# A fused attention and two-MLP kernel: a planner that counts the landing of stores, new ranks, and a warm-up on the identity

## The chip, the core and the metric

The program runs on one core of a Trainium2 chip. The metric is the device time of one execution in microseconds (us), and the kernel's figure is the median of several runs. A core has TensorE (PE) for matrix products, VectorE (DVE), ScalarE (ACT) and GpSimd (POOL) for elementwise work, and SyncE (SP), whose instruction queue issues all the transfers here. Each engine takes its own instructions strictly in the order in which they were written and waits on semaphores that the others raise. PE's results go to PSUM banks, everything else lives in SBUF.

## What is computed

```python
# q, k, v: (4 batches, 8 heads, 576 tokens, 64)
rel  = pos[:, None] - pos[None, :]
mask = (rel >= 0) & (rel < 128)                  # window of 128
s    = where(mask, q @ k.T / 8 - slope[h] * abs(rel), -1e9)
p    = exp(s - max(s)); p /= sum(p) + 1e-9
x    = (p @ v) laid out as (2304 tokens, 512)
a, b = x @ w1, x @ w2                            # 512 -> 1024
y    = (a * b) @ w3 @ w_out                      # 1024 -> 1024 -> 512
h    = maximum(y @ w_in, 0)                      # 512 -> 2048
out  = (h * h) @ w_out2                          # 2048 -> 512, fp32
```

The weights arrive as 64-bit words, and the kernel makes fp32 of them itself.

## The kernel before

**Attention** runs over 16 pairs of heads. For a pair, `qk` loads two heads of q and k and four small loads fetch v (`t_load_v`, L395). PE makes the scores (L467, two groups a pair), DVE adds the bias and takes the row's extreme (`l_min`, L435), ACT takes the exponential (L443), DVE sums and inverts (L452, L453), the rows are normalized (L254 on DVE, L252 on POOL, L256 on ACT), PE transposes them against the identity in four groups (L503), ACT copies these to SBUF (`pt`, `pl`, by the helper at L200), and PE multiplies with v (L527, then L543). Batch 0's result stays in SBUF as a high and a low half, the other batches' results are stored to `x_scr`.

**Weights.** A weight tile of 1024 KB is loaded into one of 11 buffers with the tag `u` (those of w_out into four others), and three operations make fp32 of it: ACT L330, DVE L339 (or ACT L335) and DVE L345. w3 and w_out are multiplied with each other first (64 products, L659), so that y needs one product less. The eight tiles of w1 and w2 (`w12`) are then split into a high and a low half (L200 or L260, then L203) and also stored to `m_scrc` for later. The sixteen tiles of the second MLP's weights (`in_w2io`, L843) are merged in the same manner ahead of their use: load into `u`, conversion, store to `m_scri` or `m_scro` (L849).

**Products.** Each fp32 product is three products of halves (L195 to L197). For batch 0 there are 32 units of a and b (12 matmuls of 288 columns each; `ab`) and 16 units of y. A product of a and b (L722) is split into halves too (L260, L203: `gf`, `gt`). For batches 1 to 3 and for the second MLP the products go by seven block products instead of eight (L1080 to L1082, L1131 to L1133), with sums on DVE and copies on ACT. Their first one is L1080.

**What sets the order.** Nothing is written in program order by hand. `Plan` holds some 3,100 tasks, each with a rank, the engines it may run on with a cost for each, the tasks it depends on, and the buffers it takes and gives back. `Plan.run` goes through a modelled time: of the tasks that could start within 0.1 us of the earliest it takes that of the lowest rank, puts it on an engine, and notes when its buffers come free. A dependent task on another engine starts `lat` later (3.0 for a transfer). The result is the order of every engine's instructions. On the chip only this order is left: the waits are semaphores. A buffer that a store reads is given back by the store's task (`gives`), and the tile framework makes the next user of that buffer wait for the store to have landed. Where the plan finds PE idle for over 1 us in the first 40 us, it puts in matmuls whose result nobody reads (`filler`), and it opens with a few of them (`warm`, L569).

```python
            for h in gives:
                left[h] -= 1
                last[h] = max(last[h], fin)
                if left[h] == 0:
                    pool[self.holds[h][0]].append(last[h] + 0.1)
```

Of the kernel before, what the change touches and what calls it, by code (L numbers as in the profile page):

```python
# [12 lines left out]
ALU = mybir.AluOpType  # L13


RANK = dict(w34=3, h0=-20, w12=35.93, w12s=7.96, w12l=7.68, mg=500, mgs=4, yl=8, yn=0, hs=10)
B, H, S, D = 4, 8, 576, 64
NT = B * S
DM = H * D
# [13 lines left out]
class Plan:  # L33
# [22 lines left out]
    def add(self, name, rank, where, fn, deps=(), takes=(), gives=(), keep=0):  # L56

        assert name not in self.tasks, name
        self.tasks[name] = (rank, where, fn, tuple(deps), tuple(takes), tuple(gives), keep)

    def run(self):
        tasks = self.tasks
        need = {n: len(t[3]) for n, t in tasks.items()}
        users = {}
        for n, t in tasks.items():
            for d in t[3]:
                users.setdefault(d, []).append(n)

        pool = {tag: [0.0] * c for tag, c in self.caps.items()}
        left = {h: v[1] for h, v in self.holds.items()}  # L70
        last = {h: 0.0 for h in self.holds}
        free = {}
        lock = 0.0
        end, on = {}, {}
        ready = {n for n, c in need.items() if c == 0}
        order = []
        shape = lambda n: 1 if n[:3] == "pvl" else {"qk": 1, "pv": 2}.get(n[:2], 0)
        now = 0
        while ready:
            cands = []  # L80
            for n in ready:
                rank, where, fn, deps, takes, gives, keep = tasks[n]
                t0 = 0.0
                ok = True
                for tag in {self.holds[h][0] for h in takes}:
                    p = sorted(pool[tag])
                    want = sum(self.holds[h][0] == tag for h in takes)
                    if len(p) < want + keep:
                        ok = False
                        break  # L90
                    t0 = max(t0, p[want - 1])
                if not ok:
                    continue
                best = None
                for q, w in where.items():
                    e = q.lower()
                    if e == "pe" and shape(n) != now:
                        w += self.SWITCH
                    elif e == "pe" and now:
                        rank -= self.STAY  # L100
                    t = max(t0, free.get(e, 0.0))
                    if q in "Dp":
                        t = max(t, lock)
                    for d in deps:
                        t = max(t, end[d] + (0.0 if on[d] == e else self.lat[on[d]]))
                    key = t + w + self.bias.get(q, 0.0)
                    if best is None or (key, t) < best[:2]:
                        best = (key, t, q, w)
                cands.append((best[1], rank, n, best[2], best[3]))
            assert cands, (sorted(ready)[:20], {h: (v[0], left[h]) for h, v in self.holds.items() if left[h] > 0 and any(h in tasks[n][4] for n in end)})  # L110
            t0 = min(c[0] for c in cands)
            near = [c for c in cands if c[0] <= t0 + self.LOOK]
            t, rank, n, q, w = min(near, key=lambda c: (c[1], c[0], c[2]))
            e = q.lower()
            _, _, fn, deps, takes, gives, _ = tasks[n]
            if e == "pe":
                now = shape(n)
                idle = t - free.get(e, t)
                if 1.0 < idle and t < self.FILL:
                    for tag in "tg":  # L120
                        p = pool[tag]
                        if p and min(p) <= free[e]:
                            p.remove(min(p))
                            k = f"fill{len(order)}"
                            tasks[k] = (0, {}, lambda e, tag=tag, idle=idle: self.filler(tag, int((idle - 0.4) / 0.24), 128), (), (), (), 0)
                            order.append((k, e, free[e], t - 0.4))
                            p.append(t)
                            break
            ready.remove(n)
            for h in takes:  # L130
                p = pool[self.holds[h][0]]
                p.remove(min(p))
            fin = t + w
            end[n], on[n] = fin, e
            free[e] = fin
            if q in "Dp":
                lock = fin
            for h in gives:
                left[h] -= 1
                last[h] = max(last[h], fin)  # L140
                if left[h] == 0:
                    pool[self.holds[h][0]].append(last[h] + 0.1)
            order.append((n, e, t, fin))
            for u in users.get(n, ()):
                need[u] -= 1
                if need[u] == 0:
                    ready.add(u)
        assert len(order) == len(tasks) and len(end) + sum(n[:4] == "fill" for n in tasks) == len(tasks), [n for n in tasks if n not in end][:20]
        return order
# [3 lines left out]
def fused_kernel(  # L153
# [11 lines left out]
    nc = tc.nc  # L165
# [50 lines left out]
    ident = const.tile([128, 128], F32, name="ident")  # L216
    make_identity(nc, ident)

    bw = at.tile([128, H, 256], F32, name="bw")
# [65 lines left out]
    def w_dma(kb, n=1):  # L285
        return max(0.55 * n, kb / 300.0)
# [18 lines left out]
    w34 = [None] * 4  # L305
# [89 lines left out]
    def t_load_v(m):  # L395
        b, p = divmod(m, H // 2)
        v = vt[m % 2]
        nc.sync.dma_start(
            out=v[:, :, 0:4, :].rearrange("p h c d -> p h (c d)"),
            in_=v_main[b, 2 * p:2 * p + 2].rearrange("h p c -> p h c"),  # L400
        )
        nc.sync.dma_start(
            out=v[64:128, :, 4:6, :].rearrange("p h c d -> p h (c d)"),
            in_=v_main[b, 2 * p:2 * p + 2, 0:64, 2 * D:4 * D].rearrange("h p c -> p h c"),
        )
        nc.sync.dma_start(out=v[0:64, :, 4, :], in_=v_main[b, 2 * p:2 * p + 2, 64:128, 0:D].rearrange("h p d -> p h d"))
        nc.sync.dma_start(out=v[0:64, :, 5, :], in_=v_rest[b, 2 * p:2 * p + 2].rearrange("h p d -> p h d"))
# [155 lines left out]
        b, p = divmod(m, H // 2)  # L563
        nc.sync.dma_start(out=x_scr[b][p], in_=xt[b, p])

    def p_warm(tag="t", k=4, w=256):
        t = (ps_t if tag == "t" else ps_g).tile([128, 512], F32, tag=tag, name=tag)
        for _ in range(k):
            nc.tensor.matmul(t[:, 0:w], ident, bw[:, 0, 0:w], start=True, stop=True)  # L569

    plan.filler = p_warm

# [5 lines left out]
    def add_pair(m, rank):  # L578
# [8 lines left out]
        for n in heads:  # L587
            add(f"ldq{n}", r, {"dma": w_dma(295)}, lambda e, n=n: t_load_qk(n), [f"ldq{n - 1}"] if n else [],
                [f"qk{m}"] if n % 2 == 0 else [])
        add(f"ldv{m}", r + 0.1, {"dma": w_dma(393, 2)}, lambda e: t_load_v(m), [f"ldq{heads[1]}"], [f"v{m}"])  # L590
        for n in heads:
            hold(f"s0_{n}", "s", 3)
            hold(f"s1_{n}", "s", 2)
# [879 lines left out]
```

## Time and profile before

| what | value |
|---|---|
| median of 3 runs | 838.32 us (836.11 to 838.72) |
| the profiled execution | 835.16 us, its span 833.4 us |
| PE busy | 804.7 us (97%) |
| DVE busy | 610.1 us (73%) |
| ACT busy | 469.3 us (56%) |
| transfers | 138.73 MB, mean 166 GB/s |
| KB of one load or store | q and k of a head 288, v of a pair 256 + 64 + 32 + 32, a weight tile 1024, x_scr 288, m_scr 512 |

The span is the traced part of the execution; 1.8 us of the profiled execution lie around it. A busy PE is not PE at its peak, since matmuls overlap and their ends are modelled; a stage is better read by how many units of known length it got through.

### The profile page before, as it was taken

How to read it: one execution, taken by the hardware profiler on the slowest of the kernel's cores; microseconds unless marked ns; L12 is line 12 of the kernel's file. 1: busy time of each engine (PE TensorE's matmuls, PEld its weight loads, DVE VectorE, ACT ScalarE, POOL GpSimd, SP SyncE). 2: the span in 40 equal slices, each digit the busy share in tenths (PEclk: the TensorE clock that was granted, in tenths of full speed). 3: DMA queues.
4: the chain of work that ended last, by engine and by line, in shares of the span. 5: the costliest groups of instructions: out<-in, count | busy, mean ns of one | idle time of the engine just before them, and what ended most of it. 6: DMA issues, size and time to landing. Idle time of an engine off the chain costs nothing.

```text
span 833.4 us, 17233 instructions
## 1 busy us (share of the span) xinstructions
PE 804.7 (97%) x6716; PEld 748.0 (90%) x6716; DVE 610.1 (73%) x1349; ACT 469.3 (56%) x1011; POOL 63.3 (8%) x74
## 2 busy tenths in 40 slices
PE   6999999987999999999999999999999899999998
PEld 5655659876999999999999999999999899999998
DVE  5997899983598897797489574622599898676762
ACT  5877788873332452342234475645798776566531
POOL 1010010000000200020030130000112010000000
PEclk9999999998999999999999999999999999999999
DMA  9899899876732534202133453533795755544300
GB/s 252 275 317 286 271 299 283 245 203 198 237 123 93 171 139 160 73 1 76 52 109 105 155 184 129 190 114 112 246 291 199 206 142 158 139 135 140 93 26 32
DMA packets 96960, 138.73 MB, mean 166 GB/s; under 512 B 10864, under 2 KB 74864, under 8 KB 94832
## 3 DMA queue, kind: packets, MB, share of 16 engines
q1 hardware_dynamic: 96880, 137.65, 52.9%
q8 instruction: 52, 0.85, 0.4%
q14 instruction: 28, 0.23, 0.1%
HBM read 95.81 MB, written 41.81 MB: 165 GB/s over the span
## 4 chain that ended last, share of the span: by engine, by line
PE 80%; DMA 8%; DVE 6%; ACT 3%; issue 1%; SPq 1%; POOL 0%; POOLq 0%; ACTq 0%; DVEq 0%
PE xa L1131 8%; PE xa L1133 8%; PE xa L1132 8%; PE g L659 6%; PE g L195 5%; PE g L196 5%; PE g L197 5%; PE xb L1133 4%; PE xb L1131 4%; PE xb L1132 4%; DMA m_scri<-u 3%; PE al L1080 3%; PE al L1082 3%; PE al L1081 3%; PE s L467 2%; DMA u<-in_w2io_dram 2%
## 5 line engine op out<-in xcount | busy, mean ns | idle before, releaser
L1192 DVE TENSOR_TENSOR D<-xb,D 128x384 f32<-128x384 f32 (+1 forms) x66 | 34.0, 518 | 58.4 <-PE xb L1133 30.1
L195 PE MATMUL g<-gt,wu 128*128 128x288 f32 x256 | 76.7, 300 | 0.0
L196 PE MATMUL g<-gt,wu 128*128 128x288 f32 x256 | 76.3, 298 | 0.0
L197 PE MATMUL g<-gt,wu 128*128 128x288 f32 x256 | 76.1, 297 | 0.0
L443 ACT ACTIVATE e<-e,st 128x128 f32<-128x128 f32 (+1 forms) x144 | 62.5, 438 | 13.7 <-DVE st L435 13.1
L200 ACT ACTIVATE D<-xa 128x384 f32<-128x384 f32 (+1 forms) x102 | 46.2, 454 | 38.5 <-PE xa L1133 35.2
L659 PE MATMUL g<-raw 128*128 128x512 f32 x128 | 61.0, 603 | 0.0
L1080 PE MATMUL al<-x,wc 128*128 128x288 f32 x192 | 57.1, 297 | 1.3 <-ACT d L200 1.3
L203 DVE TENSOR_TENSOR ww<-fq,ww 128x1024 fp32r<-128x1024 f32 x34 | 41.6, 1222 | 22.1 <-ACT ww L200 21.9
L200 ACT ACTIVATE ww<-fq 128x1024 fp32r<-128x1024 f32 x35 | 37.0, 1058 | 34.9 <-PE xa L1133 19.3
L1082 PE MATMUL al<-x,wc 128*128 128x288 f32 x192 | 56.7, 295 | 0.0
L1081 PE MATMUL al<-x,wc 128*128 128x288 f32 x192 | 56.6, 295 | 0.0
L200 ACT ACTIVATE ye<-g 128x288 f32<-128x288 f32 x32 | 13.1, 411 | 69.8 <-PE g L197 62.3
L1222 ACT ACTIVATE D<-D 128x384 f32<-128x384 f32 x72 | 37.0, 523 | 24.9 <-DVE D L1192 24.7
L868 DVE TENSOR_TENSOR st<-st 128x256 f32<-128x256 f32 (+1 forms) x105 | 41.7, 427 | 10.9 <-DMA st<-m_scrc 5.9
L196 PEld LDWEIGHTS g<-gt,wu 128*128 128x128 f32 x256 | 48.9, 191 | 0.0
L197 PEld LDWEIGHTS g<-gt,wu 128*128 128x128 f32 x256 | 48.8, 191 | 0.0
L195 PEld LDWEIGHTS g<-gt,wu 128*128 128x128 f32 x256 | 48.6, 190 | 0.1
L503 PEld LDWEIGHTS t<-ident,e 128*128 128x128 f32 x208 | 24.4, 142 | 26.0 <-ACT pt L200 15.9
L200 ACT ACTIVATE d<-al 128x288 f32<-128x288 f32 x71 | 28.8, 409 | 31.4 <-PE al L1082 25.2
L503 PE MATMUL t<-ident,e 128*128 128x128 f32 x208 | 36.0, 286 | 8.9 <-ACT pt L200 8.8
L435 DVE CUSTOM_DVE_ANT_0 e<-s,bw 128x192 f32<-128x192 f32 (+1 forms) x128 | 40.9, 351 | 4.8 <-PE s L467 4.5
(270 smaller groups left out, 2783.6 us busy)
## 6 DMA issues: line engine op xcount, KB each, us to landing
s_scr<-D SPq DMA_DIRECT2D x96, 192.0 KB, 2.0
u<-in_w2io_dram SPq DMA_DIRECT2D x22, 512.0 KB, 6.1
fo<-s_scr SPq DMA_DIRECT2D x20, 512.0 KB, 4.9
qk<-in_qk_dram SPq DMA_DIRECT2D x32, 288.0 KB, 5.7
st<-m_scrc SPq DMA_DIRECT2D x18, 512.0 KB, 3.7
raw<-in_w3t_dram SPq DMA_DIRECT2D x8, 1024.0 KB, 8.7
raw<-in_w_dram SPq DMA_DIRECT2D x8, 1024.0 KB, 7.2
fq<-s_scr SPq DMA_DIRECT2D x16, 512.0 KB, 5.0
```

Of the source, the lines that this page charges most:

```text
L195: nc.tensor.matmul(o, wh, xh, start=start, stop=False)
L196: nc.tensor.matmul(o, wh, xl, start=False, stop=False)
L197: nc.tensor.matmul(o, wl, xh, start=False, stop=stop)
L200: nc.scalar.activation(out=o, in_=i, func=ACTF.Copy)
L443: nc.scalar.activation(out=e, in_=e, func=ACTF.Exp, bias=st[:, 0, x:x + 1], scale=-1.0, accum_out=st[:, 1, x:x + 1],)
L659: nc.tensor.matmul(gw[fi], wl, wr, start=c == 0, stop=c == 7)
L1080: nc.tensor.matmul(o, wh, xh, start=start and c == 0, stop=False, skip_group_check=True)
L1081: nc.tensor.matmul(o, wh, xl, start=False, stop=False, skip_group_check=True)
L1082: nc.tensor.matmul(o, wl, xh, start=False, stop=c == 1, skip_group_check=True)
L1131: nc.tensor.matmul(o, wh, xh, start=start, stop=False, skip_group_check=True)
L1132: nc.tensor.matmul(o, wh, xl, start=False, stop=False, skip_group_check=True)
L1133: nc.tensor.matmul(o, wl, xh, start=False, stop=stop, skip_group_check=True)
```

## The change

Four things are edited. In `RANK`, the first pair's rank goes from -20 to -40 and the step from pair to pair from 10 to 7, so that each pair ranks lower (earlier) against the weights. In `Plan.run`, a task on the `dma` engine gives its buffers back at its end plus `lat` plus 0.5, that is 3.5 later. The four loads of v are priced as three instead of two. The matmuls of `p_warm` read the identity on both sides, 128 columns wide, instead of the identity and the bias table; the opening ones are nine of 128 columns instead of four of 256.

```diff
-RANK = dict(w34=3, h0=-20, w12=35.93, ..., yl=8, yn=0, hs=10)
+RANK = dict(w34=3, h0=-40, w12=35.93, ..., yl=8, yn=0, hs=7)
...
-                            tasks[k] = (0, {}, lambda e, tag=tag, idle=idle: self.filler(tag, int((idle - 0.4) / 0.24), 128), (), (), (), 0)
+                            tasks[k] = (0, {}, lambda e, tag=tag, idle=idle: self.filler(tag, int((idle - 0.4) / 0.24)), (), (), (), 0)
...
-                last[h] = max(last[h], fin)
+                last[h] = max(last[h], fin + (self.lat[e] + 0.5 if e == "dma" else 0.0))
...
-    def p_warm(tag="t", k=4, w=256):
+    def p_warm(tag="t", k=9):
         t = (ps_t if tag == "t" else ps_g).tile([128, 512], F32, tag=tag, name=tag)
         for _ in range(k):
-            nc.tensor.matmul(t[:, 0:w], ident, bw[:, 0, 0:w], start=True, stop=True)
+            nc.tensor.matmul(t[:, 0:128], ident, ident, start=True, stop=True)
...
-        add(f"ldv{m}", r + 0.1, {"dma": w_dma(393, 2)}, lambda e: t_load_v(m), [f"ldq{heads[1]}"], [f"v{m}"])
+        add(f"ldv{m}", r + 0.1, {"dma": w_dma(393, 3)}, lambda e: t_load_v(m), [f"ldq{heads[1]}"], [f"v{m}"])
```

As a result the order moves as a whole up to the first L1080. Before, the 64 products L659 lay among pairs 2 to 9 and sixteen units of a and b and five of y among pairs 9 to 15. Now the L659 lie among pairs 3 to 15, and all units of a, b and y of batch 0 behind the last pair. From the first L1080 on, PE's order is the same but for some exchanged neighbours in the last third.

SP's queue before, in the attention's last pairs (`u` is a weight buffer, `m_scri` the store of a merged tile, `x_scr` an attention result, `v0`, `v1` and `qk` loads for the next pairs):

```order
L393 DMA qk_2098<-in_qk_dram 64x2x576 x2
L849 DMA m_scri0_95<-u_1889 128x1024
L843 DMA u_2183<-in_w2io_dram 128x1024 x2
L564 DMA x_scr2_89<-pt_2046 128x576
L398 DMA v1_162<-in_v_main_dram 128x2x256
L402 DMA v1_162<-in_v_main_dram 64x2x128
L406 DMA v1_162<-in_v_main_dram 64x2x64
L407 DMA v1_162<-in_v_rest_dram 64x2x64
L393 DMA qk_2294<-in_qk_dram 64x2x576 x2
L849 DMA m_scri1_96<-u_1977 128x1024
L843 DMA u_2355<-in_w2io_dram 128x1024 x2
```

SP's queue of the changed kernel, at its first loads of these tiles (`xm` is the load of a whole batch of attention results for batch 1):

```order
L370 DMA m_scrc7_110<-raw_2338 128x1024
L843 DMA u_2433<-in_w2io_dram 128x1024 x2
L564 DMA x_scr3_90<-pt_2342 128x576
L843 DMA u_2489<-in_w2io_dram 128x1024 x2
L843 DMA u_2543<-in_w2io_dram 128x1024 x2
L849 DMA m_scri0_95<-u_2433 128x1024
L1027 DMA xm_2612<-x_scr1_88 128x4x576
L849 DMA m_scri1_96<-u_2489 128x1024
L849 DMA m_scri2_97<-u_2543 128x1024
L843 DMA u_2692<-in_w2io_dram 128x1024 x2
L843 DMA u_2738<-in_w2io_dram 128x1024 x2
```

Before, a load that reuses the buffer of a store stood right behind that store, with loads for the next pairs behind it; now all loads of v, q and k stand ahead of the first L843, and three stores are issued before the next load that needs one of their buffers.

DVE before, around the second sum of the last pair (L452, L453; `u` a tile of the second MLP, `gf` and `gt` the product of a and b and its halves):

```order
L722 TENSOR_TENSOR gf<-g,a_sb 128x288
L260 CAST gt<-gf 128x288
L203 TENSOR_TENSOR gt<-gf,gt 128x288
L339 TENSOR_SCALAR u<-u 128x1024
L452 TENSOR_SCALAR st_164<-st_164 128x5
L453 RECIPROCAL st_164<-st_164 128x5
L254 TENSOR_SCALAR e<-e,st_164 128x128
L254 TENSOR_SCALAR e<-e,st_164 128x192 x4
L345 SCALAR_TENSOR_TENSOR u<-u 128x1024
```

DVE of the changed kernel at the same sum (`raw` and `wu` a tile of w1 and w2 and its halves or a half of w3 times w_out):

```order
L339 TENSOR_SCALAR raw<-raw 128x1024
L345 SCALAR_TENSOR_TENSOR raw<-raw 128x1024
L260 CAST wu<-raw 128x1024
L203 TENSOR_TENSOR wu<-raw,wu 128x1024
L452 TENSOR_SCALAR st_164<-st_164 128x5
L453 RECIPROCAL st_164<-st_164 128x5
L203 TENSOR_TENSOR wu<-g,wu 128x512
L254 TENSOR_SCALAR e<-e,st_164 128x192
L339 TENSOR_SCALAR raw<-raw 128x1024
L345 SCALAR_TENSOR_TENSOR raw<-raw 128x1024
```

Eight triples L722, L260, L203 and four conversions of `u`, which stood ahead of this sum, now stand behind it, and two more tiles of w1 and w2 are converted behind it.

## Rows read from the trace of the kernel before

**Rows 1.** Busy time by stage: window, PE, PEld, DVE, ACT, POOL, granted clock, DMA, GB/s
```profile
0.00:60.00 60.00, 51.28 (x595) 34.10 (x596) 47.35 (x190) 44.80 (x141) 6.72 (x22) 1.00 0.93 283
60.00:160.00 100.00, 99.89 (x1190) 68.37 (x1189) 89.31 (x334) 79.37 (x245) 4.39 (x6) 1.00 0.91 277
160.00:217.30 57.30, 47.82 (x568) 43.36 (x566) 31.42 (x108) 29.42 (x90) 0.00 (x0) 0.94 0.70 210
217.30:239.80 22.50, 22.50 (x169) 22.50 (x170) 19.34 (x38) 7.29 (x14) 0.00 (x0) 1.00 0.52 184
239.80:300.00 60.20, 58.87 (x438) 57.97 (x437) 55.40 (x111) 24.21 (x51) 6.01 (x5) 1.00 0.41 135
...
597.00:660.00 63.00, 59.07 (x354) 57.69 (x353) 56.65 (x79) 50.81 (x82) 9.89 (x10) 1.00 0.74 237
```

**Rows 2.** Waits in SP's queue, 0 to 200 us: us in total, times, longest
```profile
SPq L843 <- DMA m_scri<-u: 21.3, 4, 6.2
```

**Rows 3.** The chain that ended last, 140 to 225 us: start us, us, what
```profile
194.23 7.10 DMA m_scri<-u
```

**Rows 4.** ACT in order of time, 199 to 203 us
```profile
200.05 1.10 ACT L330 ACTIVATE u<-u 128x1024 f32<-128x1024 f32 x1 [4.97 <-DMA u<-in_w2io_dram]
```

**Rows 5.** PE's waits, 180 to 222 us
```profile
PE t L503 <- ACT pt L200: 6.3, 3, 3.7
```

**Rows 6.** PE by stretches of 2 us: window, PE busy, granted clock, DMA, GB/s
```profile
202.00:204.00 2.00, 2.00 (x10) 0.50 0.00 0
```

**Rows 7.** PE in order of time, 239.3 to 240.1 us
```profile
239.79 0.29 PE L1080 MATMUL al<-x,wc 128*128 128x288 f32 x1
```

**Rows 8.** DVE's waits, 10 to 190 us
```profile
DVE e L435 <- PE s L467: 10.8, 11, 3.9
DVE u L339 <- DMA u<-in_w2io_dram: 3.9, 2, 2.6
DVE raw L345 <- ACT raw L330: 2.7, 2, 2.2
DVE u L345 <- DMA m_scri<-u: 2.3, 1, 2.3
```

**Rows 9.** PE in order of time: the opening matmuls
```profile
4.95 3.78 PE L569 MATMUL t<-bw,ident 128*128 128x256 f32 x8 [4.95 <-POOL bw L229]
```

**Rows 10.** POOL and DVE in order of time, first 24 us
```profile
1.16 0.30 POOL masks.py:199 TENSOR_SCALAR_AFFINE_SELECT ident<-ident 128x128 f32<-128x128 f32 x1
...
10.33 0.29 DVE L435 CUSTOM_DVE_ANT_0 e<-s,bz 128x128 f32<-128x128 f32 x1 [3.90 <-PE s L467]
```

**Rows 11.** Transfers issued in the first 2.1 us: KB each, median us to landing
```profile
qk<-in_qk_dram SPq DMA_DIRECT2D x2, 288.0 KB, 4.3
```

**Rows 12.** DVE in order of time: second sums of pairs 9 and 15
```profile
124.98 0.16 DVE L452 TENSOR_SCALAR st<-st 128x5 f32<-128x5 f32 x1
...
190.58 0.16 DVE L452 TENSOR_SCALAR st<-st 128x5 f32<-128x5 f32 x1
```

**Rows 13.** DVE, 60 to 190 us, by shape: busy us, mean ns of one
```profile
L345 DVE SCALAR_TENSOR_TENSOR raw<-raw 128x1024 uint32<-128x1024 uint32 x12 | 14.7, 1223 | 3.0 <-ACT raw L330 2.7
...
L203 DVE TENSOR_TENSOR wu<-raw,wu 128x1024 fp32r<-128x1024 f32 x7 | 8.6, 1223 | 1.0 <-ACT wu L200 0.9
...
L339 DVE TENSOR_SCALAR raw<-raw 128x1024 uint32<-128x1024 uint32 x10 | 6.9, 691 | 0.0
...
L203 DVE TENSOR_TENSOR gt<-gf,gt 128x288 fp32r<-128x288 f32 x8 | 3.7, 459 | 0.3
L722 DVE TENSOR_TENSOR gf<-g,a_sb 128x288 f32<-128x288 f32 x8 | 3.6, 454 | 0.1
...
L260 DVE CAST gt<-gf 128x288 fp32r<-128x288 f32 x8 | 2.5, 310 | 0.3
```

**Rows 14.** PE in order of time: the end of pair 9's products with v
```profile
132.27 0.51 PE L543 MATMUL a<-pt,v 64*64 64x64 f32 x18
```

**Rows 15.** The page: GB/s in 40 slices of 20.8 us
```profile
GB/s 252 275 317 286 271 299 283 245 203 198 237 123 93 171 139 160 73 1 76 52 109 105 155 184 129 190 114 112 246 291 199 206 142 158 139 135 140 93 26 32
```

More of the change, by code (lines that the diff above doesn't have):

```diff
@@ L13 @@
 ALU = mybir.AluOpType
-RANK = dict(w34=3, h0=-20, w12=35.93, w12s=7.96, w12l=7.68, mg=500, mgs=4, yl=8, yn=0, hs=10)
+RANK = dict(w34=3, h0=-40, w12=35.93, w12s=7.96, w12l=7.68, mg=500, mgs=4, yl=8, yn=0, hs=7)
 B, H, S, D = 4, 8, 576, 64
```

## Prediction

> **What bounds the kernel now.** I read the busy time by stage first. From 217.3 us on the program is one dense row of matmuls: PE is busy all of 22.5 us, 58.9 of 60.2, and in the worst later stage 59.1 of 63.0 [rows 1]. What there is to win lies before. The first 60 us have PE at 51.3 of 60, and the stretch from 160 to 217.3 at 47.8 of 57.3 with a granted clock of 0.94 on average [rows 1]. All four edits act there.
>
> Why PE stops in the second stretch is read from the queues. SP's own waits show four loads of the second MLP's weights that stood 21.3 us in all for a store out of the same buffer, 6.2 the longest [rows 2]; the chain has such a store landing after 7.10 us [rows 3]. Behind a waiting load stand the loads of v, q and k of the next pairs. ACT then comes to the conversion of that tile, 4.97 us idle for its load [rows 4], and behind this conversion on ACT stands the copy of the transposed rows, without which PE can't go on: PE waits 6.3 us on it, 3.7 once [rows 5]. After that wait the granted clock is 0.50, that is 1.2 instead of 2.4 GHz [rows 6]. So one task that the plan believed free held three engines. The first block product L1080, behind which the order stays as it is, starts at 239.79 [rows 7]; the forecast is made for this instant.
>
> The runner-up is DVE. From 60 to 160 us it is busy 89.3 of 100 while PE is at 99.9 [rows 1], and what it waits for from 10 to 190 is 10.8 us for scores, 2.7 for ACT, and 3.9 + 2.3 for tiles of the second MLP or their stores [rows 8].
>
> **The change part by part.**
>
> The warm-up. PE's first matmul waits 4.95 us for the bias table and the opening takes 3.78 us for 1024 columns [rows 9]; the scores follow at 8.73. The identity is ready at 1.16 + 0.30 = 1.46 [rows 10]. Nine matmuls of 128 columns are 1152, at the same pace 4.25 us, so they end at 5.7. The two loads of q and k, issued in the first 2.1 us, take 4.3 us to land [rows 11]; I take 6.1 for the second. So the scores start some 2.6 us earlier, and DVE's first bias, at 10.33 after a wait of 3.90 [rows 10], with them. Bounds: 0 if something else is late, 3.9 if all of the wait goes. The fillers keep their size and reading the identity instead of the table is the same form, so I cost that at nothing; PE's idle time hides it.
>
> The ranks, the landing and the price of v work together through the order. DVE sets the pace of the attention, so I count what DVE does ahead of the second sum of pair 15, at 190.58 now [rows 12]. Behind this sum go eight triples L722, L260, L203 at 0.454 + 0.310 + 0.459 = 1.223, that is 9.8 us; four conversions of second-MLP tiles at 0.691 + 1.223 = 1.914, 7.7 us; two of w1 and w2, 3.8 us; and one low half, 1.22 us [rows 13]. That is 22.5. Two small drains and four small sums move too; against them nine normalizations come ahead of it, partly from POOL, and I set these off against each other.
>
> Waits of DVE. The 3.9 + 2.3 = 6.2 us on second-MLP tiles [rows 8] go, since no such load or conversion is left ahead of the last pair. Of the scores' 10.8, 3.9 were the start, so 6.9 + 2.7 = 9.6 stay open. Scores rank ahead of L659 more often now, but PE is needed nearly as much as DVE: ahead of pair 15's end it loses only 16 units of a and b and five of y, at 22.5 / 14 = 1.607 us each [rows 1] 33.7 us. Bounds: 0, and twice 9.6. I take 6, nearer to the row than to nothing, a gain of 3.6.
>
> So the sum of pair 15 comes at 190.6 - 2.6 - 22.5 - 6.2 - 3.6 = 155.7. What follows is a pair's tail: in pair 9, undisturbed, the second sum is at 124.98 [rows 12] and the products with v end at 132.27 + 0.51 = 132.8 [rows 14], 7.8 us, and one last L659 makes it 8.7: 164.4. Then batch 0 in one piece: 32 units of a and b and 8 of y. Forty such units take 64.3. L1080 starts at 228.7, 11.1 us earlier than now.
>
> In this piece DVE does what was put off: 16 triples (19.6), eight conversions (15.3), two of w1 and w2 with their halves, and the first operands of batch 1, some 55 us of 73. It is covered, but the eight second-MLP tiles now have to be loaded, converted and stored within those 64 us. SP's first such load waits for a store of w1 and w2 two rows ahead, and its fourth for the first merged store, three stores earlier. The landings leave one to four us to the conversions on ACT, so I take 0 here and 12.9 as the far bound (the loss of 160 to 217.3, below).
>
> After L1080 PE's order is the same. In 239.8 to 300 DVE is busy 55.4 of 60.2 [rows 1], but it has the same work left as before and meets it in the same order. The exchanged neighbours near 597 to 660, where PE loses 3.9 us in all [rows 1], I cost at 0, bounds 3.9 gained and 3.9 lost.
>
> The sum: 835.16 - 11.1 = 824.1 for an execution like the profiled one. The median of the runs shown is 3.2 us above it, so the forecast is 838.3 - 11.1 = 827.2.
>
> Two rules bear on this. A store of 512 KB took 7.10 us here [rows 3]. The Trainium skill, DMA: Bandwidth & Descriptors, section Anatomy of one DMA — SWDGE (gpsimd) path, gives about 2.0 us plus the bytes at 436 GB/s, an estimated 3.2 us for this one, on another issue path. By that figure the waits that go would be worth half, and the forecast 830; the measurement decides.
>
> The clock stays at 1.00 in the first 60 us with PE busy 51.3 of 60 [rows 1] and falls to 0.50 only after the 3.7 us wait [rows 5, 6]. The Trainium skill, TensorE: Matmul & The Clock Gate, section on the HAM clock gate, has idle time bring TensorE back to 1.2 GHz, which speaks against giving PE fewer products among the first pairs. Should it fall there, ten us at the lower level would cost five and leave 832; by the rows it doesn't.
>
> **The rivals.**
>
> More is gained. If PE is never late for DVE, the other 6 us go too: 821. For it: the first pairs have almost nothing but their own matmuls ahead of their scores. Against it: PE's own work up to that point is nearly as long as DVE's.
>
> The loads set the pace. Pairs are now asked for sooner. Ahead of pair 8's q and k the queue holds eight pairs' q and k, seven v, four tiles of w3, four of w_out and one store, 16.8 MB with them; the three first slices, at 252, 275 and 317 GB/s, moved 17.6 MB in 62.5 us [rows 15]. DVE wants these scores at about 65 us. If the queue's waits for buffers cost it a tenth to a fifth of that rate, the attention comes 6 to 11 us later: 833 to 838. The trace shows the queue blocked often, but with more bytes ahead.
>
> The stall moves instead of going. Loads of the second MLP's tiles wait for stores in the dense piece too, and behind them on SP stand the stores of y, whose two buffers PE needs. If they come late, ACT stands at a conversion ahead of its copies exactly as now. The price is what it costs now: 57.3 - 47.8 = 9.5 us idle and 0.06 x 57.3 = 3.4 us of clock, 12.9 [rows 1]. With the waits of DVE kept in full (3.6) that is 827.2 + 16.5 = 844, slower. It decides from the point where a tile lands more than about four us after the copy ahead of its conversion.
>
> The gain is given back. Batch 1's stage hangs on DVE, and if its weights or loads come no sooner, PE waits there for what it won: 836 to 840.
>
> **How the numbers follow.** The forecast has 50%, with its own range from 822 to 832; more gained 20%, the loads 14%, the gain given back 7%, the stall moved 9%. The range that leaves out no more than 2 in 10 runs from 816 (no waits, the whole 3.9 at the start, and the late stage's idle time gone) to 838 (the loads at their worst). A measurement of this kernel can tell about 0.3%, 2.5 us, from no change. Faster takes the first two and most of the loads' case, 81%; within 0.3% most of the case given back and the rest of the loads', 9%; slower 10%.
>
> **What would show it.** The first scores at about 6 us and DVE's first bias at 7.7; the second sum of pair 15 at 151 to 160; no L843 waiting for a store ahead of it; L1080 at 224 to 234 with PE busy and its clock at 1.00 in the 64 us before it; and a distance from L1080 to the end of 593.6 us as before. It is wrong if DVE's waits for scores or ACT's for transfers add up to over 20 us before 160, if PE idles in the dense piece, or if that last distance grows.

## The result, and the profile after

The changed kernel takes 826.26 us (median of 4 runs, 825.79 to 828.39) against 838.52 of the kernel before (4 runs, 836.11 to 842.69); the ratio is 0.985, with a 95% interval of [0.981, 0.990], so 1.5% faster. The forecast was 827.2. The profiled execution is the longest of the four, 828.39 us with a span of 826.6.

First the busy time by stage, after, in the columns of [rows 1]:

```profile
0.00:60.00 60.00, 53.54 (x789) 40.16 (x790) 49.58 (x243) 49.61 (x174) 3.82 (x18) 1.00 0.96 253
60.00:160.00 100.00, 98.01 (x1195) 61.34 (x1195) 89.37 (x344) 84.05 (x269) 1.60 (x4) 1.00 0.90 282
160.00:217.30 57.30, 57.30 (x459) 54.72 (x458) 38.82 (x64) 21.50 (x35) 0.00 (x0) 1.00 0.81 275
217.30:239.80 22.50, 22.33 (x166) 21.79 (x165) 21.18 (x46) 7.95 (x15) 0.00 (x0) 1.00 0.36 116
239.80:300.00 60.20, 59.09 (x436) 57.86 (x435) 55.89 (x112) 26.35 (x50) 5.74 (x4) 1.00 0.40 135
597.00:660.00 63.00, 59.10 (x365) 57.72 (x365) 55.38 (x76) 50.36 (x77) 13.31 (x10) 0.97 0.73 225
```

From 160 to 217.3 PE is busy throughout and the granted clock is 1.00, where before it was 47.8 of 57.3 at 0.94. In exchange PE idles a little more from 60 to 160 (2.0 us against 0.1). The last row has a new low clock, to which I come at the end.

The waits that answer to [rows 2, 4 and 5], in the order SP, ACT (150 to 240 us) and PE (100 to 260 us, all that there are); columns as there: total, times, longest:

```profile
SPq L843 <- DMA m_scri<-u: 2.7, 2, 2.3
```

```profile
ACT u L330 <- DMA u<-in_w2io_dram: 2.1, 4, 0.8
```

```profile
PE s L467 <- issue: 0.3, 1, 0.3
PE g L195 <- DVE gf L722: 0.2, 1, 0.2
```

SP's loads stand 2.7 us for a merged store in place of 21.3, ACT's conversions find their tiles 0.8 us late at the worst in place of 4.97, and PE doesn't wait for the copy `pt` any more.

The instants that the prediction named: PE's opening and first scores (against [rows 9]), DVE's second sums (first and last start, against [rows 12]), and the first L1080 (against [rows 7]):

```profile
1.52 4.21 PE L569 MATMUL t<-ident 128*128 128x128 f32 x18 [1.52 <-POOL ident masks.py:199]
5.66 2.23 PE L467 MATMUL s<-qk 64*64 64x128 f32 x32
```

```profile
L452 DVE TENSOR_SCALAR st<-st x32: 151/165/172, 11.2 to 157.2; 128x4 f32<-128x4 f32 x16, 128x5 f32<-128x5 f32 x16
```

```profile
L1080 PE MATMUL al<-x,wc x22: 292/296/401, 230.3 to 259.8; 128*128 128x288 f32 x22
```

L1080 comes at 230.3 in place of 239.8, 9.5 us earlier. The distance from there to the end grew by 2.7 us, which leaves 6.8 between the two profiled executions (835.16 and 828.39). The medians differ by 12.3, since this execution is 2.1 us above its own median and the one before was 3.4 below its own.

The chain that ended last, by engine, reads as follows on the page after; before, DMA had 8% and PE 80%:

```profile
PE 89%; DVE 6%; ACT 2%; DMA 1%; issue 1%; POOL 0%; SPq 0%; DVEq 0%; POOLq 0%; ACTq 0%
```

### The profile page after: what moved, and what is told of

The parts are those of the page before. It is cut to its first block, busy times and chain, and to the rows that moved or that the text cites. A ratio compares the mean times of both kernels' runs of the same rounds, so it can differ in the third digit from the quotient of the medians.

```text
span 826.6 us, 17260 instructions
## 1 busy us (share of the span) xinstructions
PE 807.8 (98%) x6732; PEld 750.2 (91%) x6732; DVE 612.3 (74%) x1359; ACT 467.4 (57%) x1007; POOL 60.3 (7%) x68
## 4 chain that ended last, share of the span: by engine, by line
PE 89%; DVE 6%; ACT 2%; DMA 1%; issue 1%; POOL 0%; SPq 0%; DVEq 0%; POOLq 0%; ACTq 0%
PE xa L1131 8%; PE xa L1133 8%; PE xa L1132 8%; PE g L659 6%; PE g L195 6%; PE g L196 6%; PE g L197 6%; PE xb L1131 4%; PE xb L1133 4%; PE xb L1132 4%; PE s L467 3%; PE al L1080 3%; PE al L1082 3%; PE al L1081 3%; PE t L503 2%; PE xc L1131 2%
## 5 line engine op out<-in xcount | busy, mean ns | idle before, releaser
L196 PE MATMUL g<-gt,wu 128*128 128x288 f32 x256 | 75.7, 296 | 0.0
L195 PE MATMUL g<-gt,wu 128*128 128x288 f32 x256 | 75.6, 295 | 0.0
L197 PE MATMUL g<-gt,wu 128*128 128x288 f32 x256 | 75.4, 295 | 0.0
L443 ACT ACTIVATE e<-e,st 128x192 f32<-128x192 f32 (+1 forms) x144 | 62.2, 435 | 9.1 <-DVE st L435 8.8
L659 PE MATMUL g<-raw 128*128 128x512 f32 x128 | 62.5, 603 | 0.2
L203 DVE TENSOR_TENSOR ww<-fq,ww 128x1024 fp32r<-128x1024 f32 x34 | 41.6, 1222 | 24.2 <-ACT ww L200 23.8
L1080 PE MATMUL al<-x,wc 128*128 128x288 f32 x192 | 57.5, 299 | 1.1 <-ACT d L200 1.1
L196 PEld LDWEIGHTS g<-gt,wu 128*128 128x128 f32 x256 | 48.3, 189 | 0.0
L197 PEld LDWEIGHTS g<-gt,wu 128*128 128x128 f32 x256 | 48.2, 188 | 0.0
L195 PEld LDWEIGHTS g<-gt,wu 128*128 128x128 f32 x256 | 48.1, 188 | 0.0
L467 PE MATMUL s<-qk 64*64 64x128 f32 (+2 forms) x768 | 38.2, 287 | 4.6 <-issue 1.9
```

Of the source, the lines that this page charges most:

```text
L195: nc.tensor.matmul(o, wh, xh, start=start, stop=False)
L196: nc.tensor.matmul(o, wh, xl, start=False, stop=False)
L197: nc.tensor.matmul(o, wl, xh, start=False, stop=stop)
L467: nc.tensor.matmul(HD[2 * m + r]["s"][g][o, c:c + w], t[h, 0, 64 * q:64 * q + 64], t[h, 1, 64 * k:64 * k + w], start=True, stop=True,)
L659: nc.tensor.matmul(gw[fi], wl, wr, start=c == 0, stop=c == 7)
L1080: nc.tensor.matmul(o, wh, xh, start=start and c == 0, stop=False, skip_group_check=True)
```

## The experiments

The runs come in three groups, each beside its own runs of the kernel before, whose medians are 838.62, 838.57 and 839.23 us. Ratios are to these, with 95% intervals. "L1080" is the start of the first block product and "sum" the last pair's second sum, both of the one profiled execution (before: 239.8 and 190.6).

### Each edit by itself

**Only the warm-up.**

```diff
...
-    def p_warm(tag="t", k=4, w=256):
+    def p_warm(tag="t", k=9):
...
-            nc.tensor.matmul(t[:, 0:w], ident, bw[:, 0, 0:w], start=True, stop=True)
+            nc.tensor.matmul(t[:, 0:128], ident, ident, start=True, stop=True)
```

> The kernel before with the warm-up of the changed kernel alone; every other instruction stands where it stood. First theory: the scores start when q and k land, some 2.6 us earlier, and as DVE sets the pace of the attention this is carried through: 836 us against 838.5. Rival: the stall on the second MLP's tiles later soaks up the earlier start, and the time is that of before within 0.5 us; DVE's first bias is early, L1080 is not.

838.09 us, ratio 0.998 [0.996, 1.000]; sum 189.4, L1080 239.2. SP's wait of L843 for `m_scri` stays at 21.1 us. The scores start 3 us earlier, and 0.6 us of it are left at L1080. The time is close to the rival's, but it isn't the stall that soaks the start up: nearly all of it is gone by the third pair, long before 160 us. The second sums of this pair, number 2 when counted from 0, before and in this run:

```profile
33.80 0.16 DVE L452 TENSOR_SCALAR st<-st 128x5 f32<-128x5 f32 x1
```

```profile
33.43 0.16 DVE L452 TENSOR_SCALAR st<-st 128x5 f32<-128x5 f32 x1
```

In pair 0 this sum was still 3.1 us earlier (12.48 against 15.54). In between PE waits longer for q and k of the next pairs, and the granted clock falls. PE's wait for `qk` from 5 to 60 us, before and in this run, and then the stretch of this run where the clock falls to 0.50, that is 1.2 of 2.4 GHz (in the kernel before it is 1.00 there):

```profile
PE s L467 <- DMA qk<-in_qk_dram: 0.7, 2, 0.5
```

```profile
PE s L467 <- DMA qk<-in_qk_dram: 2.6, 2, 1.6
```

```profile
18.00:20.00 2.00, 1.93 (x35) 0.86 1.06 428
20.00:22.00 2.00, 2.00 (x46) 0.50 0.64 258
```

The last two lines have the columns of [rows 6].

**Only the landing.**

```diff
-                last[h] = max(last[h], fin)
+                last[h] = max(last[h], fin + (self.lat[e] + 0.5 if e == "dma" else 0.0))
```

> The kernel before with the landing of stores priced in the plan, the old ranks, the old price of v and the old warm-up. Units of a, b and y stay among the last pairs (18 in place of 21), four in place of five loads L843 stand ahead of the last v. First theory, the stall is what there was to win: the loads stand three to six rows behind the stores of their buffers, so SP waits about half as long (10 of 21 us), L1080 starts at 232 and the time is 831. Rival, the ranks are the gain (DVE has 2.4 us less ahead of the last pair's second sum here, against 23 in the changed kernel): 836 or more.

824.73 us, ratio 0.982 [0.979, 0.985]: better than either theory had it, and the lowest median of all runs. Its interval overlaps that of the changed kernel, so it beats before but isn't told apart from the change as a whole. SP, PE (100 to 260 us), the second sums and L1080:

```profile
SPq L843 <- DMA m_scri<-u: 5.6, 2, 2.9
```

```profile
PE s L467 <- DVE st L435: 1.1, 1, 1.1
PE t L503 <- ACT pt L200: 0.6, 1, 0.6
```

```profile
L452 DVE TENSOR_SCALAR st<-st x32: 157/163/171, 13.4 to 183.0; 128x4 f32<-128x4 f32 x16, 128x5 f32<-128x5 f32 x16
```

```profile
L1080 PE MATMUL al<-x,wc x28: 290/296/302, 227.5 to 259.2; 128*128 128x288 f32 x28
```

The last pair's sum comes at 183.0, 26 us later than in the changed kernel, and L1080 still 2.8 us sooner. So the time of that sum doesn't set L1080.

**Only the ranks.**

```diff
-RANK = dict(w34=3, h0=-20, ..., hs=10)
+RANK = dict(w34=3, h0=-40, ..., hs=7)
```

> The kernel before with the new ranks of the pairs alone: no landing in the plan, old price of v, old warm-up. No load L843 stands ahead of the last v, and DVE has as little ahead of the last second sum as in the changed kernel. First theory (what ends the stall is that these loads stand behind the attention, by whatever edit): all of the gain but the start's 2.6 us, 829 to 830. Rival, the landing's price is what keeps the stall out of the dense piece: the loads wait for their stores there, L1080 stays near 238 and the time at 836 or more.

842.73 us, ratio 1.005 [1.002, 1.007]: slower. The sum comes at 157.8, as early as in the changed kernel, and L1080 at 241.4. Stages (columns as above), SP's wait, PE's largest from 100 to 320 us, and one of ACT:

```profile
0.00:60.00 60.00, 44.92 (x722) 34.09 (x723) 45.97 (x231) 45.64 (x163) 3.82 (x18) 1.00 0.98 253
60.00:160.00 100.00, 97.11 (x1223) 61.51 (x1223) 91.14 (x354) 87.42 (x278) 1.65 (x4) 1.00 0.89 275
160.00:217.30 57.30, 55.23 (x399) 47.94 (x398) 32.76 (x50) 18.32 (x30) 0.00 (x0) 1.00 0.78 258
```

```profile
SPq L843 <- DMA m_scri<-u: 14.9, 4, 6.8
```

```profile
PE g L195 <- ACT ye L200: 2.1, 1, 2.1
PE al L1080 <- ACT d L200: 2.1, 4, 0.6
```

```profile
ACT ye L200 <- DMA y_scr<-ye: 6.8, 1, 6.8
```

PE idles 15.1 us in the first 60, against 8.7 before. It has fewer products to fill in there, 2.1 us of L659 in place of 18.2, and waits 5.1 us for the copies `pt` and 3.2 for DVE's bias. And the loads still wait 14.9 us, now in the dense piece, with the stores of y behind them: ACT stood 6.8 us for one of y's buffers and PE 2.1 us for that copy. This is the rival "the stall moves", in the order that has no landing price.

**The changed kernel without the landing price** (its other three edits stay).

```diff
-                last[h] = max(last[h], fin + (self.lat[e] + 0.5 if e == "dma" else 0.0))
+                last[h] = max(last[h], fin)
```

> The changed kernel without the landing of stores in the plan. First theory: the same as the changed kernel within 1 us, 826 to 827, since the ranks already put the loads L843 behind the attention. Rival (the landing's price keeps the stall away): 832 or more, with SP waiting over 10 us for m_scri and ACT for w2io between 160 and 230 us.

837.46 us, ratio 0.998 [0.996, 1.000]: nearly the whole gain is gone. Sum 157.7, L1080 234.0, SP's L843 waits 16.5 us in all for `m_scri`. A further part is lost behind L1080, which the 60 us from L1080 on show, first of this run, then of the changed kernel:

```profile
234.00:294.00 60.00, 54.80 (x393) 52.40 (x392) 56.03 (x109) 17.19 (x37) 8.48 (x5) 1.00 0.44 144
```

```profile
230.30:290.30 60.00, 58.89 (x431) 57.35 (x431) 55.76 (x113) 23.09 (x49) 4.29 (x3) 1.00 0.41 135
```

There are 38 matmuls fewer. By the unit of [rows 1], 1.607 us for twelve, that is an estimated 5.1 us. The loads stand close behind their stores again, in the same place of the program; SP's queue of this run has

```
L849 DMA m_scri0_95<-u_2433 128x1024
L843 DMA u_2612<-in_w2io_dram 128x1024 x2
L849 DMA m_scri1_96<-u_2489 128x1024
L849 DMA m_scri2_97<-u_2543 128x1024
L843 DMA u_2692<-in_w2io_dram 128x1024 x2
```

where in the changed kernel three stores go ahead of the next such load.

### What the landing price avoids

**The store made shorter, the order kept.** The kernel before, its merged tiles stored by a quarter and read back four times over.

```diff
-        nc.sync.dma_start(out=m_scr[k, m], in_=f(flat(raws.pop((k, m)))))
+        t = f(flat(raws.pop((k, m))))
+        w = 256 if k == "i" else 1024
+        nc.sync.dma_start(out=m_scr[k, m][:, 0:w], in_=t[:, 0:w])
...
-        nc.sync.dma_start(out=t[:, 0:1024], in_=m_scr[k, m])
+        w = 256 if k == "i" else 1024
+        nc.sync.dma_start(
+            out=t[:, 0:1024].rearrange("p (r n) -> p r n", n=w),
+            in_=m_scr[k, m][:, 0:w].unsqueeze(1).broadcast_to([128, 1024 // w, w]),
+        )
```

> The kernel before, its order untouched on every engine, but each merged tile of the first second-MLP matrix (m_scri) is stored with 256 of its 1024 columns, and read back with these four times over, so 3/4 of that stored data are left out. Only the landing of eight stores gets shorter. Second theory, formed after the four runs: the stall is the wait for these landings and nothing else, so with a landing of some 3 us in place of 7 SP's wait for m_scri falls from 21 us to under 8, L1080 comes at 231 to 234, and the time is 830 to 833. Rival (the order itself, units of a and b among the last pairs, is what costs): SP's wait falls but L1080 stays within 2 us of 239.8, 837 or more.

834.01 us, ratio 0.994 [0.992, 0.996]; L1080 236.1. Neither theory's ranges were met, and the edit missed its aim: SP's wait shrank only from 21.3 to 17.9 us, since a quarter of the bytes doesn't land in anything like a quarter of the time. The DMA issues, before and in this run (KB, median us to landing):

```profile
m_scri<-u SPq DMA_DIRECT2D x8, 512.0 KB, 5.9
```

```profile
m_scri<-u SPq DMA_DIRECT2D x8, 128.0 KB, 4.1
```

L1080 came 3.7 us sooner with 3.4 us less of SP's wait, which fits the theory but is too small a step to decide. What the run tells of the landing stands at the end.

**The store taken from another buffer, the order kept.** This takes away just the tie between the store and the next load. It is the kernel before, word for word in its order on every engine; the merged data of four tiles are left out.

```diff
-        nc.sync.dma_start(out=m_scr[k, m], in_=f(flat(raws.pop((k, m)))))
+        t = f(flat(raws.pop((k, m))))
+        if k == "i" and m < 4:
+            t = f(xt[0, m].rearrange("p a s -> p (a s)"))[:, 0:1024]
+        nc.sync.dma_start(out=m_scr[k, m], in_=t)
```

> The kernel before with its order of instructions untouched on every engine. The stores of the first four merged weight tiles (m_scri 0 to 3) send the two halves of a pair of batch 0's attention result, which stay in SBUF, in place of the merged tile: the same 512 KB, at the same place in the queue, but not out of the weight buffer, so the next load into that buffer waits for the conversion alone (these four tiles' data is lost, so the second MLP computes with other numbers). First theory: the loss of 160 to 217 us is the wait of a load for the landing of a store out of its own buffer, and the price in the planner gains by getting around just that. Then with before's order SP's loads wait under 6 us for stores in place of 21, PE is busy at least 55 of the 57.3 us, L1080 comes at 228 to 231 and the median is 825 to 829. Rival: the loads are late through the queue and the other transfers, whatever buffer the store reads; then the conversion still waits some 4 us for its tile, L1080 stays at 235 to 240 and the median at 833 to 838.

828.73 us, ratio 0.989 [0.987, 0.992]; sum 182.1, L1080 229.9. No L843 waits for a merged store at all. What is left of the stall is one load that comes late, in ACT's and PE's waits from 140 to 240 us, the stage from 160 us as a whole, and the ten us where it falls:

```profile
ACT u L330 <- DMA u<-in_w2io_dram: 5.6, 2, 4.7
```

```profile
PE g L195 <- ACT a_sb L200: 3.5, 1, 3.5
PE s L467 <- DVE st L435: 0.3, 1, 0.3
```

```profile
160.00:217.30 57.30, 53.76 (x631) 51.00 (x631) 37.03 (x117) 31.93 (x93) 0.00 (x0) 0.97 0.75 241
```

```profile
190.00:200.00 10.00, 10.00 (x119) 9.64 (x119) 4.77 (x6) 2.88 (x8) 0.00 (x0) 1.00 0.28 94
200.00:210.00 10.00, 6.46 (x37) 6.22 (x36) 3.06 (x5) 1.86 (x3) 0.00 (x0) 0.83 1.01 326
210.00:217.30 7.30, 7.30 (x57) 7.30 (x56) 4.96 (x10) 2.43 (x5) 0.00 (x0) 1.00 0.62 195
```

With no change of order, and the same bytes, 1.1% [0.8, 1.3] of the time goes. The first theory holds for most of the loss: it was the wait of a load for the landing of a store out of its own buffer. L1080 and the median came within the first theory's ranges and far from the rival's. Two details did not: PE is busy 53.8 of 57.3 us where at least 55 was expected, and one conversion still waits 4.7 us for its tile, as the rival had it. The landing price alone gained 1.8%, clearly more than this; it also keeps that last pause away (PE busy 56.1 of 57.3 at 1.00), but no run here takes the rest apart.

**The price on the weight stores alone, and on all others alone.**

```diff
+                last[h] = max(last[h], fin + (self.lat[e] + 0.5 if n[:2] == "ms" else 0.0))
```

> The kernel before with the landing priced in the plan for the weight stores alone (tasks msc, msi, mso; 16 + 3 stores), old ranks, old price of v, old warm-up. Up to 590 us its order is that of only_landing. Second theory: all of the gain of only_landing, 824 to 826, since the rest of the priced stores only reorders the last third. Rival (the stores of the block products' sums share the gain): 829 or more, with the distance from L1080 to the end over 597.

```diff
+                last[h] = max(last[h], fin + (self.lat[e] + 0.5 if e == "dma" and n[:2] != "ms" else 0.0))
```

> The kernel before with the landing price on all stores but those of weight tiles (attention results, y and the later ones), the complement of the run that prices the weight stores alone (826.0). First theory: the gain of 160 to 217 us belongs to the weight stores; the order is before's up to the last pairs and the four loads wait some 21 us as in before; 836 to 839, not distinguishable. Rival: the late stages gain from the price on the other stores, as the 1.3 us between the two landing runs so far might suggest; 833 to 836 with L1080 still at 239.

The first takes 826.00 us, 0.985 [0.983, 0.988], L1080 227.0; the second 836.46 us, 0.997 [0.996, 0.999], L1080 239.6, and its SP waits as before:

```profile
SPq L843 <- DMA m_scri<-u: 20.1, 4, 6.9
```

The price on the stores `m_scrc`, `m_scri` and `m_scro` is the gain, nearly all of it. What the others add is some 0.3%, at the edge of what can be told: the second run's median lies within the first theory's range and close to the rival's.

### Combinations

**Before with landing and warm-up**, **the changed kernel with the old ranks**, **with v priced at two**, and **with the old warm-up**; their edits are lines of the change, put in or taken back.

```diff
-RANK = dict(w34=3, h0=-40, ..., hs=7)
+RANK = dict(w34=3, h0=-20, ..., hs=10)
...
-        add(f"ldv{m}", r + 0.1, {"dma": w_dma(393, 3)}, ...
+        add(f"ldv{m}", r + 0.1, {"dma": w_dma(393, 2)}, ...
```

> The kernel before with the landing priced and the new warm-up; old ranks and old price of v. Second theory: with the stall gone the earlier start is carried through, 2.6 us below only_landing's 824.7, so 822, and 4 us below the changed kernel. Rival: DMA sets the pace of the first 60 us and the early start is lost there, 824.7 as without it.

> The changed kernel with the old ranks: landing, price of v and warm-up are in. Second theory: the ranks bring nothing by themselves and cost about 2 us, since they put 34 us of products behind the last pair that lay among the pairs before; 822 to 825, below the changed kernel's 826.3. Rival (the ranks help once the landing is priced): 828 or more.

> The changed kernel with the loads of v priced at two as before; landing price, new ranks and new warm-up stay. The runs so far give 826.7 for landing and warm-up and 829.7 for these with the price of v. First theory: the price of v costs some 3 us where the landing is priced, whatever the ranks; then this one is at 822 to 825, level with the best so far (824.7). Rival: the ranks and the price of v act on the same thing, the early pairs against the weights, so that with the new ranks the price of v changes nothing; 825 to 828, as the changed kernel.

> The changed kernel with the old warm-up, which waits for the bias table; ranks, landing and price of v stay. With the stall gone, a later start could show at last. First theory: the start is soaked up by the attention's waits whatever the order, as the run of landing with warm-up (826.7) against landing alone (824.7) suggests; no difference from the changed kernel, 824.5 to 828, L1080 at 229 to 232. Rival: in the changed order DVE is behind from the start and the 2.6 us of the prediction show; 828.5 to 830, L1080 2 to 3 us later than 230.3.

| kernel | median us | ratio | sum | L1080 |
|---|---|---|---|---|
| landing and warm-up | 826.71 | 0.985 [0.982, 0.987] | 184.5 | 229.0 |
| change, old ranks | 829.67 | 0.989 [0.987, 0.991] | 187.1 | 230.5 |
| change, old price of v | 831.00 | 0.992 [0.989, 0.995] | 151.6 | 231.9 |
| change, old warm-up | 830.75 | 0.990 [0.988, 0.993] | 159.7 | 232.8 |

The old warm-up in the changed order costs what the prediction had given it, in the instants of the one profiled execution: the sum comes 2.5 us later than in the changed kernel and L1080 2.5. The median is 4.5 us higher, but the intervals of the two ratios overlap (0.990 [0.988, 0.993] and 0.985 [0.981, 0.990]), so the times alone don't settle it. In before's order and in that of landing with warm-up the same edit brought nothing: landing and warm-up were expected at 822 by the theory and at 824.7 by the rival, and took 826.71, with pair 2's second sum 0.9 us later than with the landing alone. As the stall is gone there, this too says that the early start is lost among the first pairs. The old ranks came out slower than the changed kernel by their median, against the theory and as the rival had it; these intervals overlap as well. The old price of v gave the earliest sum of all and a later L1080, and both theories had it too fast: in its first 60 us PE is busy 49.42, 4.1 less than after, and the granted clock is 0.97.

```profile
0.00:60.00 60.00, 49.42 (x774) 38.63 (x775) 49.26 (x247) 49.16 (x175) 3.82 (x18) 0.97 0.94 266
```

This fall of the clock goes with the price of v. With the new warm-up and v priced at two (only the warm-up, landing and warm-up, change with the old price of v) PE waits 2.4 to 2.7 us for `qk` in the first 60 us and the clock of this stage is 0.97. With the new warm-up and v priced at three (the change, the change without the landing price, the change with the old ranks) it waits at most 1.9 us and the clock is 1.00. These are single executions, and the price of v was never run by itself.

Over all: the seven kernels with the price on the weight stores took 824.7 to 831.0 us, the five without it whose stores are those of before (before, only the warm-up, only the ranks, the price on the other stores, the change without it) 836.5 to 842.7. Within the first group the order differs much and the time by 0.8%; the intervals of neighbours overlap, and what sets their order among themselves I leave open. It isn't what is left of SP's wait: the change with the old ranks has none of it and L1080 at 230.5, the price on the weight stores alone has 8.0 us of it and L1080 at 227.0.

## Why the prediction was right, and where not

**The bound: right.** That one task held three engines is shown by the run with the store from another buffer. It has before's order, and of the 12.9 us of idle time and low clock from 160 to 217.3 it keeps 3.5 + 1.7 = 5.2. There the sum comes 8.5 us earlier and L1080 9.9.

**The warm-up, 2.6 us: right in the changed kernel only.** Scores at 5.66 (said: about 6), DVE's first bias at 8.0 (said: 7.7), 2.5 us at the sum and at L1080 against the old warm-up. By itself it is worth nothing measurable, since in the trace of that run PE's waits for q and k and a fall of the clock take it back among the first pairs. The prediction had weighed such a fall in the first 60 us and set it aside by its rows; in the changed kernel the clock stayed at 1.00, in three of its relatives it did not.

**The second sum at 155.7: right as an instant, wrong as the lever.** It came at 157.2. Of its terms, DVE's other waits were too small: 6 was said, and from 10 to 157 us DVE waited 8.2 us for scores and exponentials and 2.2 for tiles of w3 and w_out, which the prediction had at nothing:

```profile
DVE st L452 <- ACT e L443: 4.2, 3, 2.1
DVE e L435 <- PE s L467: 4.0, 7, 0.9
DVE raw L339 <- DMA raw<-in_w_out_dram: 1.9, 1, 1.9
DVE raw L339 <- DMA raw<-in_w3t_dram: 0.3, 1, 0.3
```

That is 4.4 us more, of which 1.5 show at the sum; the other terms must have made up the rest, and to that extent the instant was luck. The tail took 8.5 us to the first unit (said: 8.7) and the forty units, from 165.7 to 230.3, took 64.6 (said: 64.3).

The step "the ranks, the landing and the price of v work together through the order", which sought the gain in what DVE does ahead of this sum, failed as a cause. Sums at 157.8 and 157.7 go with L1080 at 241.4 and 234.0, and one at 183.0 with 227.5. The account shows why the number came out all the same. The forecast brought the sum 34.9 us forward and put 33.7 of units and 0.9 of L659 behind it, 34.6: together nothing but 0.3. Its gain of 11.1 is the rest. From the sum to L1080 the kernel before took 239.8 - 190.6 = 49.2 us, and 73.0 - 34.6 = 38.4 was allowed for the same work, 10.8 less. Unsaid, that is the stall: the forecast came out because it took the work behind the sum to run dense, and not because of what it moved ahead of it. On which side of the sum the stall lies hangs on the order: with the store from another buffer 8.5 us of it came off ahead of the sum. The gain is read more simply from what PE idles until L1080: before 8.7 + 0.1 + 9.5 = 18.3 us and 3.4 of clock [rows 1], after 6.5 + 2.0 + 0 = 8.5, with the landing alone 8.3 + 0.6 + 1.2 = 10.1, and with the ranks alone 15.1 + 2.9 + 2.1 up to 217.3. Of the 13.2 us between before and after, 9.5 are won at L1080. PE was also busy 9.3 us in place of 7.9 with matmuls that nobody reads; the other 2.3 I can't place.

**No stall in the dense piece: right, but by a margin that one line made.** I took 0 of 12.9 because three stores stand ahead of the next load. That was so, and it is the landing price that puts them there: without it, at the same ranks, the loads stood 16.5 us. The rival "the stall moves" describes the change without this edit. I gave it 9%, with a time of 844 where the run took 837.46, and didn't see what held it off.

**The distance behind L1080: 596.3 us, 593.6 before.** The prediction had named a growing distance as a sign of being wrong, and it grew by 2.7 us. The order there was said to cost nothing, and the stages support it: the 2.7 us are mostly one episode of low clock. The stretch 420 to 480 us behind L1080, after and with the landing alone (distance 594.2):

```profile
650.30:710.30 60.00, 60.00 (x501) 60.00 (x501) 46.74 (x51) 41.59 (x48) 2.96 (x1) 0.98 0.58 163
```

```profile
647.50:707.50 60.00, 60.00 (x511) 60.00 (x510) 48.78 (x51) 41.42 (x48) 2.50 (x1) 1.00 0.59 163
```

**The other rivals.** "More is gained" needed DVE's waits for scores and ACT to go, and they stayed. "The loads set the pace" shows weakly: PE waited 1.4 us for `qk` from 5 to 200 us. "Given back" needs batch 1 to take the gain, and the 60 us behind L1080 have PE busy 58.89, as before.

## What to carry to other kernels

A scheduler that hands out buffers has to count a buffer as taken until the transfer that reads it has landed, not until it is issued; one line of that was as good as the whole gain here. A forecast for this reordered kernel would have been better made on the engine that sets the end, by its idle time, and not on an instant in the middle of the program: work moved behind such an instant comes back. Of several edits that go together, each wants the question what the others do without it: of the three tried alone here, one gave the whole gain, one nothing that can be told, and one cost 0.5%.

## What was not expected of the hardware

**The landing of a store shrinks far less than its size here.** 512 KB took 5.9 us in the median before and 3.7 in the changed kernel, 128 KB 4.1 us with before's order. Store by store the eight took 4.6, 6.9, 6.1, 6.6, 7.1, 2.8, 5.7 and 2.9 us before, and 4.0, 6.7, 6.1, 4.7, 4.3, 2.2, 2.4 and 2.0 with a quarter of the bytes: three hardly sooner, the others by 0.6 to 3.3. The Trainium skill, DMA: Bandwidth & Descriptors, section Anatomy of one DMA — SWDGE (gpsimd) path, has a fixed 2.0 us and the bytes at 436 GB/s, an estimated 2.3 us for 128 KB and 3.2 for 512, on another issue path; the medians are above it, and the rows are far apart for the same size. What else is under way may count as much as the bytes; no run isolates it.

**The same pause of PE may or may not lower the clock.** In the late stage PE waits 2.1 us for `ww` both in the changed kernel and with the landing alone. After this the granted clock fell to 0.50, that is 1.2 GHz, in the changed kernel's profiled execution, and stayed at 1.00 with the landing alone. The changed kernel first, in the columns of [rows 1]:

```profile
646.00:648.00 2.00, 0.30 (x3) 0.09 (x1) 2.00 (x3) 1.12 (x2) 0.00 (x0) 1.00 0.45 125
648.00:650.00 2.00, 1.64 (x11) 1.64 (x12) 2.00 (x3) 2.00 (x3) 0.00 (x0) 0.81 0.89 263
650.00:652.00 2.00, 2.00 (x11) 2.00 (x11) 1.72 (x2) 0.87 (x1) 0.00 (x0) 0.50 1.04 290
652.00:654.00 2.00, 2.00 (x17) 2.00 (x17) 0.00 (x0) 1.23 (x2) 0.00 (x0) 0.84 1.19 313
```

```profile
642.00:644.00 2.00, 0.97 (x9) 0.76 (x7) 2.00 (x4) 0.79 (x2) 0.00 (x0) 1.00 0.56 164
644.00:646.00 2.00, 0.95 (x8) 0.95 (x9) 2.00 (x2) 2.00 (x3) 0.00 (x0) 1.00 1.01 298
646.00:648.00 2.00, 2.00 (x20) 2.00 (x19) 2.00 (x3) 1.54 (x3) 0.00 (x0) 1.00 0.80 204
```

At 0.50 eleven matmuls go by in 2 us in place of twenty. The episode costs about 2 us, which is most of the distance that grew; why it fell in the one and not in the other stays open.
